# Softplus of the first feed-forward as one ScalarE function, and its inverse root on VectorE

## The chip, the cores and the metric

The kernel runs as one program on one core of a Trainium2 chip. The metric is the device time of one execution in microseconds (us); the time before is the median of 3 runs. PE is the matmul engine, ACT ScalarE, DVE VectorE, POOL GpSimd, SP SyncE, whose queue issues nearly all DMAs. Each engine works through its own instructions in the order in which the program has them; a wait at the head of one engine's queue holds everything behind it on that engine.

## What is computed

Causal attention with a cumulative bias (4 x 8 heads, 576 positions, width 64), then two feed-forward layers over 2304 tokens of width 512, cut here to what the change touches:

```python
h = x @ w_in                                               # 512 -> 2048
g = np.maximum(h, 0.0) + np.log1p(np.exp(-np.abs(h)))      # softplus
y = g @ w_out                                              # 2048 -> 512
rms = np.sqrt(np.mean(y * y, axis=-1, keepdims=True) + 1e-06)
xn = y / rms * rms_g
out = (silu(xn @ w_gate) * (xn @ w_val)) @ w_out2          # 512 -> 1536 -> 512
```

## The kernel before

Three parts follow each other on PE: attention, the first feed-forward, the second. Weights arrive as 64-bit numbers and are turned into fp32 on the core, chunk by chunk, during the first two parts. Every fp32 product is made of three matmuls on high and low halves (`mm3`, L773): high times high, high times low, low times high. So each activation that feeds a matmul is needed as a high half (`gh`, rounded to the matmul type) and a low half (`gl`, value minus high half).

**First feed-forward.** Tokens go in 6 tiles of 384. A step is one tile and one block of 128 of the 2048 hidden columns. There are 96 steps: a first pass of 6 blocks for each tile, then a second of 10 blocks for each tile, whose sums are added to those of the first (read back from DRAM, `y_load`). On PE a step has two blocks of 12 matmuls of 128x384: `h` (L778), from x, and `Y` (L828), which multiplies the softplus by w_out into four PSUM banks.

Between h and Y a step passes through nine small functions: `m1_abs` (ACT, |h|), `m1_exp` (ACT), `m1_ln` (ACT, ln(1+e)), `m1_u` (ACT, 1+e rounded), `m1_d` (DVE, the rounding error of it), `m1_g` (DVE, max(h,0) minus the error, the last reader of h in PSUM), `m1_add` (DVE), `m1_gh` (ACT) and `m1_gl` (POOL in the first 6 steps, DVE after that). h has three PSUM buffers, so h of step i+3 needs step i's to be read out.

**What sets the order.** All events of the two feed-forwards carry a place, in units of steps, and are sorted by it (`at`, L995; the table `OFF1`, L19). h of step i stands at i-0.57, Y at i+2.57. So on PE the blocks run h(i+3), Y(i), h(i+4), Y(i+1) and so on. Each engine's queue has its events in the order of these places. The same sort places:

- the conversion of weight chunks: `w_fetch` (SP), `w_conv_a` (ACT, two operations, the first an Abs), `w_conv_d` (DVE, three), `w_conv_p` (POOL), then `w_hi` and `w_lo`; one chunk per 1.49 steps in the first third, one per 2.9 steps later;
- the x tiles: `x_load` (SP), and `x_split` for four column blocks of the next tile (ACT `xh`, then POOL `xl`);
- the norm of a finished tile t, whose places are counted from e, the place of its last Y: `m1_evac` (DVE adds the sums of the first pass), `m1_ss`, `m1_sh` (POOL and DVE, squares), `m1_ssum` (two matmuls), `m1_inv` (inverse root), `m1_xn` (POOL multiplies, SP stores). `m1_inv` uses one DVE operation, Ln and Exp on ACT and one Newton step of four POOL operations.

In SP's queue the `y_load`s of tile t+1 stand behind the first `m1_xn` stores of tile t. The **second feed-forward** has 72 iterations of 24 matmuls (`m2_gv`) and 9 (`m2_out`), with `m2_act` between them (a Sigmoid on ACT, three DVE operations).

Of the kernel before, what the change touches and what calls it, by code (L numbers as in the profile page):

```python
# [10 lines left out]
I32 = mybir.dt.int32  # L11
# [3 lines left out]
AF = mybir.ActivationFunctionType  # L15
ALU = mybir.AluOpType
AX = mybir.AxisListType
PSUM = bass.MemoryType.PSUM
OFF1 = {  # L19
    "h": -0.57067,  # L20
    "A": -0.10511,
    "X": 0.37619,
    "LN": 0.46084,
    "U": 0.37819,
    "D": 0.52100,
    "G": 0.93713,
    "AD": 0.93913,
    "GH": 1.47301,
    "GL": 1.54335,
    "Y": 2.56558,  # L30
    "CF": -0.42676,
    "CA": 2.13954,
    "CD": 2.14154,
# [123 lines left out]
def attention_moe_kernel(ctx, tc, q, k, v, s, w_in, w_out, w_gate, w_val, w_out2, rms_g, out):  # L157
    nc = tc.nc
    B, H, S, D = q.shape
# [9 lines left out]
    NTILE = NT // T  # L169
# [6 lines left out]
    FA = 6  # L176
# [12 lines left out]
    pools = {}  # L189
# [13 lines left out]
    def f32(ap):  # L203
        return ap.bitcast(F32)
# [36 lines left out]
    def w_conv_a(ph, c):  # L241
        raw = raws[ph, c, "d"].bitcast(I32).rearrange("p (n t) -> p n t", t=2)
        pool = pools["cur"] if "m1" not in pools and CONV.index((ph, c)) % 2 else conv
        ur = pool.tile([P, 2, 512], I32, tag="ur", name="ur", bufs=1)
        u, r3 = ur[:, 0], ur[:, 1]
        nc.scalar.activation(out=f32(u), in_=f32(raw[:, :, 1]), func=AF.Abs)
        nc.scalar.activation(out=r3, in_=raw[:, :, 0].bitcast(U32), func=AF.Copy, scale=2.0 ** -29)
        st["cv", ph, c] = u, r3

# [51 lines left out]
    st = {}  # L301
# [486 lines left out]
    def m1_tile(tag, bufs, dt=F32):  # L788
        return pools["m1"].tile([P, T], dt, tag=tag, name=tag, bufs=bufs)

    def m1_abs(i):
        e = st["e", i] = m1_tile("e", 2)
        nc.scalar.activation(out=e, in_=st["h", i], func=AF.Abs)

    def m1_exp(i):
        e = st["e", i]
        nc.scalar.activation(out=e, in_=e, func=AF.Exp, scale=-1.0)

    def m1_ln(i):
        l = st["l", i] = m1_tile("l", 2)  # L800
        nc.scalar.activation(out=l, in_=st["e", i], func=AF.Ln, bias=1.0)  # L801

    def m1_u(i):
        u = st["u", i] = m1_tile("u", 1)
        nc.scalar.activation(out=u, in_=st["e", i], func=AF.Copy, bias=1.0)

    def m1_d(i):
        e = st["e", i]
        nc.vector.scalar_tensor_tensor(out=e, in0=st.pop(("u", i)), scalar=-1.0, in1=e, op0=ALU.add, op1=ALU.subtract)  # L809

    def m1_g(i):
        e = st["e", i]
        nc.vector.scalar_tensor_tensor(out=e, in0=st.pop(("h", i)), scalar=0.0, in1=e, op0=ALU.max, op1=ALU.subtract)  # L813

    def m1_add(i):
        l = st["l", i]
        nc.vector.tensor_tensor(out=l, in0=l, in1=st.pop(("e", i)), op=ALU.add)  # L817

    def m1_gh(i):
        gh = st["gh", i] = m1_tile("gh", 3, F32R)  # L820
        nc.scalar.activation(out=gh, in_=st["l", i], func=AF.Copy)  # L821

    def m1_gl(i):
        gl = st["gl", i] = m1_tile("gl", 3, F32R)
        eng = nc.gpsimd if i < FA else nc.vector
        eng.tensor_tensor(out=gl, in0=st.pop(("l", i)), in1=f32(st["gh", i]), op=ALU.subtract)  # L826

    def m1_y(i):  # L828
        v, _, f = STEPS[i]
# [32 lines left out]
    def ss_tile(tag, dt=F32, w=T):  # L862
        return pools["m1"].tile([P, T if tag == "sh" else 512], dt, tag=tag, name=tag, bufs=1)[:, 0:w]
# [25 lines left out]
    def m1_inv(t):  # L889
        o = st.pop(("ss", t))  # L890
        ms, z, w = ss_tile("sq"), ss_tile("acc"), ss_tile("sh")
        if t == NTILE - 1:
            nc.scalar.preload_act_table_set("natural_log_exp_and_others")
        nc.vector.tensor_scalar(out=ms, in0=o[:, 0:T], scalar1=1.0 / DM, scalar2=1e-6, op0=ALU.mult, op1=ALU.add)
        nc.scalar.activation(out=z, in_=ms, func=AF.Ln)
        nc.scalar.activation(out=z, in_=z, func=AF.Exp, scale=-0.5)
        nc.gpsimd.tensor_tensor(out=w, in0=z, in1=z, op=ALU.mult)
        nc.gpsimd.tensor_tensor(out=w, in0=w, in1=ms, op=ALU.mult)
        nc.gpsimd.tensor_scalar(out=w, in0=w, scalar1=-0.5, scalar2=1.5, op0=ALU.mult, op1=ALU.add)
        nc.gpsimd.tensor_tensor(out=z, in0=z, in1=w, op=ALU.mult)  # L900
        st["inv", t] = z

    def m1_xn(t, a):
# [63 lines left out]
    with tc.manual_schedule():  # L967
# [21 lines left out]
        with ExitStack() as es0:  # L989
            pools["ps"] = es0.enter_context(tc.tile_pool(name="ps", bufs=1, space=PSUM, reuse_waits="tile"))  # L990
            pools["wb"] = es0.enter_context(tc.tile_pool(name="wb", bufs=1, reuse_waits="tile"))
            pools["m1"] = es0.enter_context(tc.tile_pool(name="m1", bufs=1, reuse_waits="tile"))
            evs = []

            def at(x, fn, *args):  # L995
                evs.append((x, len(evs), fn, args))

            NS = range(len(STEPS))
            for i in NS:
                for nm, fn in (("h", m1_h), ("A", m1_abs), ("X", m1_exp), ("LN", m1_ln), ("U", m1_u), ("D", m1_d),  # L1000
                               ("G", m1_g), ("AD", m1_add), ("GH", m1_gh), ("GL", m1_gl), ("Y", m1_y)):
                    if nm != "h" or i > 1:
                        at(i + OFF1[nm], fn, i)
            CONV1 = (("CF", w_fetch), ("CA", w_conv_a), ("CD", w_conv_d), ("CP", w_conv_p))
            SPLIT = (("CH", w_hi), ("CL", w_lo))
            x = OFF1["P0"]
            for ph, c in [(1, c) for c in range(NA, 2 * F1)] + [(2, c % (3 * F2)) for c in range(NA + N2, NA + 3 * F2)]:
                if x < len(NS) or ph == 1:
                    for nm, fn in CONV1 + (SPLIT if ph == 1 or c < NA else (("CS", w_store),)):
                        at(x + OFF1[nm], fn, ph, c)  # L1010
                x += OFF1["PR"] if ph == 1 else OFF2["CV"]
            for v in sorted({STEPS[i][0] for i in NS}):
                i = min(i for i in NS if STEPS[i][0] == v)
                t, n = v % NTILE, FA if v < NTILE else F1 - FA
                if v > 0:
                    for a in range(KD):
                        x = i + OFF1["xs"] + OFF1["xt"] * a
                        at(x + OFF1["xl"], x_load, v, a)
                        at(x, x_split, v, a, nc.gpsimd)
                e = i + n - 1 + OFF1["Y"]  # L1020
                for a in range(KD):
                    at(e + 0.001 * (a + 1), m1_evac, v, a)
                if v < NTILE:
                    continue
                for a in range(KD):
                    at(e - 1.5 + 0.2 * a, y_load, t, a)
                x = "5" if t == NTILE - 1 else ""
                for a in range(KD):
                    at(e + OFF2["ss"] + OFF2["sr"] * a, m1_ss, t, a)
                    at(e + OFF2["xn" + x] + OFF2["xr" + x] * a, m1_xn, t, a)  # L1030
                at(e + OFF2["sh" + x], m1_sh, t)
                at(e + OFF2["sm" + x], m1_ssum, t)
                at(e + OFF2["iv" + x], m1_inv, t)
            for a in range(KD):
                at(OFF2["s0"] + a - 1.8, n_load, 0, a)
                at(OFF2["s0"] + a, x_split, 0, a, nc.vector, True)
            for c in range(NA, 3 * F2):
                x = OFF2["L0"] + OFF2["LR"] * c
                at(x + OFF2["WL"], w_load, 2, c)
                at(x + OFF2["WH"], w_hi, 2, c)  # L1040
                at(x + OFF2["WO"], w_lo, 2, c)
            e = F1 * NTILE
            for i in range(NTILE * F2):
                t, f = divmod(i, F2)
                x = e + (OFF2[f"g{i}"] if i < 2 else OFF2["G"] + 1.5 * i)
                at(x, m2_gv, t, f)
                at(e + OFF2[f"a{i}"] if i < 2 else x + OFF2["a"], m2_act, t, f)
                x = e + OFF2["G"] + 1.5 * (i + OFF2["lag"]) + OFF2["o"]
                at(x, m2_out, t, f)
                if f == F2 - 1:  # L1050
                    at(x + 0.01, m2_evac, t)
                if t + 1 < NTILE and 4 <= f < 8:
                    at(x + 0.3, n_load, t + 1, f - 4)
                if t + 1 < NTILE and 6 <= f < 10:
                    at(x, x_split, t + 1, f - 6, nc.vector, True)
            evs.sort(key=lambda x: x[:2])
            for _, _, fn, args in evs:
                fn(*args)
# [29 lines left out]
```

## Time and profile before

| | |
|---|---|
| time, median of 3 runs (lowest, highest) | 1173.48 us (1172.21, 1176.06) |
| span of the profiled execution, first to last instruction | 1171.5 us |
| what the profiled execution has beside its span | not in the profile; the median is 2.0 us above the span |
| busy: PE, DVE, ACT, POOL | 1108.0, 731.3, 560.5, 474.8 us |
| first feed-forward, about | 279 to 723 us |
| second feed-forward, about | 710 to 1166 us |

The profile's page gives busy time by engine, then the span in 40 slices of 29.3 us with one digit for each (tenths busy; PEclk is the granted clock of PE in tenths). The window rows give, for a stretch in us from the span's start, its length and for PE, PEld (weight loads), DVE, ACT and POOL the busy time and, as (x...), the number of instructions, then the granted clock, the DMA share and GB/s. The wait rows give who waited <- for whom: total us, times, longest. The group rows give line, engine, operation, output<-input, shape, count | busy us, mean ns | idle before it and what ended that. The rows in order of time give start, duration, engine, line, operation and, in brackets, the idle time before it and what ended it. Matmuls overlap in the pipeline, so a matmul of 0.33 us can start every 0.17 us: the distance between starts is what counts.

### The profile page before, as it was taken

To read this page: it belongs to the slowest core of one execution; us is meant where nothing else is said; L and a number is where in the kernel's file an instruction comes from. 1 tells how busy PE (TensorE), PEld (TensorE's weight loads), DVE (VectorE), ACT (ScalarE), POOL (GpSimd) and SP (SyncE) were. 2 spreads that over 40 slices of the span, in tenths; PEclk is the share of its full clock that TensorE was granted. 3 is DMA by queue.
4 is the path that set the end of the run, shared out by engine and by line. 5 is a ranking of instruction groups with operands and counts; after the bars stand their busy time and mean duration, and the time that the engine had idled before them with its cause. 6 is when DMAs were issued, how large, how long until landed. Compare 5 with 4: busy or idle time off the path is not lost.

```text
span 1171.5 us, 19408 instructions
## 1 busy us (share of the span) xinstructions
PE 1108.0 (95%) x7428; PEld 1021.9 (87%) x7428; DVE 731.3 (62%) x1170; ACT 560.5 (48%) x1203; POOL 474.8 (41%) x404
## 2 busy tenths in 40 slices
PE   5889999997998989999999999999999999999998
PEld 4767777777988889999998999999999999999997
DVE  6788888722899998799898995343332332333322
ACT  2545656544777877776766765431211212112111
POOL 5687766644655551357767766650000000000000
PEclk9988988888999999999989999999999999999999
DMA  8556888533434433323323134231010010010000
GB/s 176 140 144 159 207 204 214 148 100 109 132 127 128 137 113 104 117 86 104 95 91 104 56 95 125 80 101 41 14 39 4 14 41 14 6 37 14 27 1 28
DMA packets 126972, 107.59 MB, mean 92 GB/s; under 512 B 67008, under 2 KB 112704, under 8 KB 126816
## 3 DMA queue, kind: packets, MB, share of 16 engines
q1 hardware_dynamic: 126848, 106.36, 31.5%
q8 instruction: 58, 0.95, 0.3%
q14 instruction: 34, 0.28, 0.1%
q0 software_dynamic: 32, 0.00, 0.0%
HBM read 80.36 MB, written 25.83 MB: 91 GB/s over the span
## 4 chain that ended last, share of the span: by engine, by line
PE 59%; DVE 25%; issue 4%; DMA 4%; ACT 4%; POOL 3%; SPq 0%; DVEq 0%; POOLq 0%; ACTq 0%
DVE gl L826 4%; PE g L776 4%; PE g L775 4%; PE v L774 4%; PE v L775 4%; PE v L776 4%; PE g L774 4%; PE t L505 3%; DVE ur L253 3%; DVE l L817 3%; PE o L950 3%; PE o L951 3%; DVE ur L255 3%; PE s L449 3%; PE o L949 3%
## 5 line engine op out<-in xcount | busy, mean ns | idle before, releaser
L775 PE MATMUL y<-gl,w 128*128 128x384 f32 x384 | 131.5, 342 | 14.9 <-DVE gl L826 12.4
L263 POOL TENSOR_TENSOR wf<-ur 128x512 int32<-128x512 int32 x68 | 94.5, 1389 | 122.2 <-DVE ur L257 48.7
L934 DVE TENSOR_TENSOR u<-g,u 128x384 f32<-128x384 f32 x71 | 39.5, 557 | 158.6 <-ACT u L933 158.6
L774 PE MATMUL y<-gh,w 128*128 128x384 f32 x384 | 129.8, 338 | 2.2 <-DVE yt L853 1.8
L776 PE MATMUL y<-gh,w 128*128 128x384 f32 x384 | 129.4, 337 | 0.0
L936 ACT ACTIVATE gh<-l 128x384 fp32r<-128x384 f32 x72 | 37.9, 527 | 155.9 <-DVE l L935 155.9
L933 ACT ACTIVATE u<-g 128x384 f32<-128x384 f32 x71 | 34.8, 491 | 151.6 <-PE g L776 151.6
L472 DVE TENSOR_REDUCE mc<-s 128x1 f32<-128x128 f32 (+4 forms) x160 | 76.7, 537 | 31.6 <-PE s L457 25.9
L775 PE MATMUL g<-xl,w 128*128 128x384 f32 x284 | 95.5, 336 | 0.7 <-DVE xl L768 0.7
L776 PE MATMUL g<-xh,w 128*128 128x384 f32 x284 | 95.8, 337 | 0.0
L774 PE MATMUL g<-xh,w 128*128 128x384 f32 x284 | 95.6, 337 | 0.0
L776 PE MATMUL v<-xh,w 128*128 128x384 f32 x284 | 94.9, 334 | 0.0
L774 PE MATMUL v<-xh,w 128*128 128x384 f32 x284 | 94.9, 334 | 0.0
L775 PE MATMUL v<-xl,w 128*128 128x384 f32 x284 | 94.9, 334 | 0.0
L809 DVE SCALAR_TENSOR_TENSOR e<-u,e 128x384 f32<-128x384 f32 x96 | 77.6, 808 | 26.9 <-ACT l L801 26.9
L775 PE MATMUL h<-xl,w 128*128 128x384 f32 x256 | 87.4, 341 | 3.9 <-POOL xl L771 3.9
L775 PEld LDWEIGHTS y<-gl,w 128*128 128x128 f32 x384 | 72.6, 189 | 21.2 <-DVE gl L826 17.9
L826 DVE TENSOR_TENSOR gl<-l,gh 128x384 fp32r<-128x384 f32 x90 | 88.3, 981 | 4.5 <-ACT gh L821 1.0
L774 PE MATMUL h<-xh,w 128*128 128x384 f32 x256 | 87.5, 342 | 1.2 <-DVE e L813 1.2
L776 PE MATMUL h<-xh,w 128*128 128x384 f32 x256 | 86.8, 339 | 0.0
L817 DVE TENSOR_TENSOR l<-l,e 128x384 f32<-128x384 f32 x96 | 80.4, 837 | 3.7
L522 ACT ACTIVATE e<-t 128x448 f32<-128x448 f32 (+2 forms) x128 | 56.4, 506 | 54.5 <-PE t L515 54.2
(178 smaller groups left out, 3094.8 us busy)
## 6 DMA issues: line engine op xcount, KB each, us to landing
raw<-in_moe_w_out_dram SPq DMA_DIRECT2D x28, 512.0 KB
raw<-in_moe_w_in_dram SPq DMA_DIRECT2D x16, 512.0 KB
raw<-in_moe_w_gate_dram SPq DMA_DIRECT2D x12, 512.0 KB
raw<-in_moe_w_val_dram SPq DMA_DIRECT2D x12, 512.0 KB
wf<-wf SPq DMA_DIRECT2D x24, 256.0 KB
wl<-wf SPq DMA_DIRECT2D x24, 256.0 KB
xr<-x SPq DMA_DIRECT2D x28, 192.0 KB
qn<-in_q_dram SPq DMA_DIRECT2D x16, 288.0 KB
```

The lines of the kernel that those rows point to most:

```text
L253: nc.vector.tensor_scalar(out=f32(u), in0=f32(u), scalar1=2.0 ** -15, scalar2=122880.0, op0=ALU.max, op1=ALU.min)
L263: nc.gpsimd.tensor_tensor(out=w.bitcast(I32), in0=u, in1=r3, op=ALU.add)
L472: nc.vector.reduce_max(out=o, in_=x, axis=AX.X, negate=True)
L522: nc.scalar.activation(out=st["e", p][:, hd, c:c + w], in_=st["t", p, bk][hd][:, 0:w], func=AF.Exp)
L774: nc.tensor.matmul(o, wh, xh, start=start, stop=False)
L775: nc.tensor.matmul(o, wh, xl, start=False, stop=False)
L776: nc.tensor.matmul(o, wl, xh, start=False, stop=stop)
L809: nc.vector.scalar_tensor_tensor(out=e, in0=st.pop(("u", i)), scalar=-1.0, in1=e, op0=ALU.add, op1=ALU.subtract)
L817: nc.vector.tensor_tensor(out=l, in0=l, in1=st.pop(("e", i)), op=ALU.add)
L826: eng.tensor_tensor(out=gl, in0=st.pop(("l", i)), in1=f32(st["gh", i]), op=ALU.subtract)
L934: nc.vector.tensor_tensor(out=u, in0=g, in1=u, op=ALU.mult)
L936: nc.scalar.activation(out=gh, in_=l, func=AF.Copy)
```

## The change

Three edits go together. First, h is read twice from PSUM by the ACT function Softplus, once into `l` (fp32) and once into `gh`; `m1_gl` subtracts them on DVE in all 96 steps. The other seven functions go. Places: h at i-0.57, the softplus at i+0.02, gl at i+0.30, Y at i+1.57, a step earlier than before. Second, `m1_inv` starts from a bit pattern and makes three Newton steps, all eleven operations on DVE. Third, the Abs of `w_conv_a` becomes a DVE operation (a mask of the sign bit) in the first feed-forward; in attention it stays on ACT.

```diff
 OFF1 = {
-    "h": -0.57067,
-    "A": -0.10511,
...
-    "Y": 2.56558,
+    "h": -0.57,
+    "SP": 0.02,
+    "GL": 0.30,
+    "Y": 1.56558,
...
-        nc.scalar.activation(out=f32(u), in_=f32(raw[:, :, 1]), func=AF.Abs)
+        if "m1" in pools:
+            nc.vector.tensor_scalar(out=u, in0=raw[:, :, 1], scalar1=0x7FFFFFFF, scalar2=None, op0=ALU.bitwise_and)
+        else:
+            nc.scalar.activation(out=f32(u), in_=f32(raw[:, :, 1]), func=AF.Abs)
...
-    def m1_abs(i):
...
+    def m1_sp(i):
+        h = st.pop(("h", i))
         l = st["l", i] = m1_tile("l", 2)
...
         gh = st["gh", i] = m1_tile("gh", 3, F32R)
-        nc.scalar.activation(out=gh, in_=st["l", i], func=AF.Copy)
+        nc.scalar.activation(out=l, in_=h, func=AF.Softplus)
+        nc.scalar.activation(out=gh, in_=h, func=AF.Softplus)
...
-        eng = nc.gpsimd if i < FA else nc.vector
-        eng.tensor_tensor(out=gl, in0=st.pop(("l", i)), in1=f32(st["gh", i]), op=ALU.subtract)
+        nc.vector.tensor_tensor(out=gl, in0=st.pop(("l", i)), in1=f32(st["gh", i]), op=ALU.subtract)
...
-        if t == NTILE - 1:
-            nc.scalar.preload_act_table_set("natural_log_exp_and_others")
         nc.vector.tensor_scalar(out=ms, in0=o[:, 0:T], scalar1=1.0 / DM, scalar2=1e-6, op0=ALU.mult, op1=ALU.add)
-        nc.scalar.activation(out=z, in_=ms, func=AF.Ln)
-        nc.scalar.activation(out=z, in_=z, func=AF.Exp, scale=-0.5)
-        nc.gpsimd.tensor_tensor(out=w, in0=z, in1=z, op=ALU.mult)
-        nc.gpsimd.tensor_tensor(out=w, in0=w, in1=ms, op=ALU.mult)
-        nc.gpsimd.tensor_scalar(out=w, in0=w, scalar1=-0.5, scalar2=1.5, op0=ALU.mult, op1=ALU.add)
-        nc.gpsimd.tensor_tensor(out=z, in0=z, in1=w, op=ALU.mult)
+        nc.vector.tensor_scalar(out=z.bitcast(I32), in0=ms.bitcast(I32), scalar1=-0.5, scalar2=1597463007.0,
+                                op0=ALU.mult, op1=ALU.add)
+        for _ in range(3):
+            nc.vector.tensor_tensor(out=w, in0=z, in1=z, op=ALU.mult)
+            nc.vector.scalar_tensor_tensor(out=w, in0=w, scalar=-0.5, in1=ms, op0=ALU.mult, op1=ALU.mult)
+            nc.vector.scalar_tensor_tensor(out=z, in0=w, scalar=1.5, in1=z, op0=ALU.add, op1=ALU.mult)
```

ACT where the first feed-forward begins, before; `e_4322` and `e_4335` belong to steps 0 and 1, `xh` is the split of the second x tile:

```order
L577 ACTIVATE xz_4276<-o0_4280 128x384
L793 ACTIVATE e_4322<-h_4229 128x384
L797 ACTIVATE e_4322<-e_4322 128x384
L805 ACTIVATE u_4325<-e_4322 128x384
L801 ACTIVATE l_4327<-e_4322 128x384
L793 ACTIVATE e_4335<-h_4208 128x384
L797 ACTIVATE e_4335<-e_4335 128x384
L805 ACTIVATE u_4340<-e_4335 128x384
L801 ACTIVATE l_4355<-e_4335 128x384
L821 ACTIVATE gh_4357<-l_4327 128x384
L770 ACTIVATE xh_4362<-xr_4319 128x384
```

The same place in the changed kernel:

```order
L573 ACTIVATE xz_4276<-o0_4280 128x384
L791 ACT_TABLE_LOAD
L791 ACTIVATE l_4322<-h_4229 128x384
L792 ACTIVATE gh_4323<-h_4229 128x384
L791 ACTIVATE l_4333<-h_4208 128x384
L792 ACTIVATE gh_4334<-h_4208 128x384
L766 ACTIVATE xh_4368<-xr_4319 128x384
```

Eight operations that alternate with three on DVE became four that read PSUM and nothing of DVE; a table load stands ahead of them. The program has three table loads: at its start, here, and before the first Sigmoid (before: four, two of them around the last tile's inverse root).

POOL around the inverse root of tile 0 (tile `acc_7078`), before; `xl` are the third and fourth column block of the next x tile, `yt<-yt,acc` is `m1_xn`:

```order
L263 TENSOR_TENSOR wf_7022<-ur_6981 128x512
L771 TENSOR_TENSOR xl_7027<-xr_6927,xh_7026 128x384
L771 TENSOR_TENSOR xl_7027<-xr_6975,xh_7026 128x384
L897 TENSOR_TENSOR sh_7079<-acc_7078 128x384
L898 TENSOR_TENSOR sh_7079<-sh_7079,sq_7077 128x384
L899 TENSOR_SCALAR sh_7079<-sh_7079 128x384
L900 TENSOR_TENSOR acc_7078<-acc_7078,sh_7079 128x384
L905 TENSOR_TENSOR yt_6643<-yt_6643,acc_7078 128x384
```

The same place in the changed kernel:

```order
L259 TENSOR_TENSOR wf_6611<-ur_6575 128x512
L767 TENSOR_TENSOR xl_6616<-xr_6533,xh_6615 128x384
L873 TENSOR_TENSOR yt_6261<-yt_6261,acc_6620 128x384
L767 TENSOR_TENSOR xl_6616<-xr_6569,xh_6615 128x384
L873 TENSOR_TENSOR yt_6263<-yt_6263,acc_6620 128x384
```

The places of the norm count from Y, which went a step earlier, those of the x split do not: the first `m1_xn` now stands ahead of the fourth `xl`.

DVE around the inverse root of tile 2, before (a few rows of three steps; `sq<-o0` is all that DVE does of it):

```order
L817 TENSOR_TENSOR l_8009<-l_8009,e_7989 128x384
L809 SCALAR_TENSOR_TENSOR e_8041<-u_8051,e_8041 128x384
L826 TENSOR_TENSOR gl_8071<-l_8009,gh_8068 128x384
L894 TENSOR_SCALAR sq_8089<-o0_8047 128x384
L813 SCALAR_TENSOR_TENSOR e_8041<-x1_7996,e_8041 128x384
```

The same place in the changed kernel, up to the first of three Newton steps:

```order
L796 TENSOR_TENSOR gl_7435<-l_7431,gh_7432 128x384
L240 TENSOR_SCALAR ur_7465<-raw_7357 128x512
L249 TENSOR_SCALAR ur_7465<-ur_7465 128x512
L251 TENSOR_SCALAR ur_7465<-ur_7465 128x512
L253 SCALAR_TENSOR_TENSOR ur_7465<-raw_7357,ur_7465 128x512
L862 TENSOR_SCALAR sq_7480<-o0_7437 128x384
L863 TENSOR_SCALAR acc_7481<-sq_7480 128x384
L866 TENSOR_TENSOR sh_7482<-acc_7481 128x384
L867 SCALAR_TENSOR_TENSOR sh_7482<-sh_7482,sq_7480 128x384
L868 SCALAR_TENSOR_TENSOR acc_7481<-sh_7482,acc_7481 128x384
```

The last three stand there twice more, then gl of the next step: eleven operations in one piece, and for this tile a chunk's conversion of four right ahead of them.

## Rows read from the trace of the kernel before

**Rows 1.** The page: busy time, and two lines of the slices.

```profile
PE 1108.0 (95%) x7428; PEld 1021.9 (87%) x7428; DVE 731.3 (62%) x1170; ACT 560.5 (48%) x1203; POOL 474.8 (41%) x404
...
DVE  6788888722899998799898995343332332333322
...
PEclk9988988888999999999989999999999999999999
```

**Rows 2.** Windows: five stretches of the two feed-forwards.

```profile
278.50:298.00 19.50, 17.93 (x84) 17.29 (x85) 8.39 (x13) 10.34 (x23) 11.31 (x10) 0.85 0.54 167
298.00:440.00 142.00, 129.22 (x708) 123.47 (x708) 133.82 (x190) 112.66 (x238) 78.52 (x58) 0.99 0.40 127
440.00:580.00 140.00, 139.83 (x804) 139.05 (x804) 120.02 (x181) 99.82 (x210) 66.68 (x57) 1.00 0.31 96
580.00:710.00 130.00, 122.15 (x676) 119.24 (x675) 118.36 (x159) 90.16 (x188) 86.98 (x73) 0.97 0.30 94
730.00:1160.00 430.00, 430.00 (x2268) 403.29 (x2267) 136.11 (x247) 93.72 (x186) 35.76 (x31) 1.00 0.09 29
```

**Rows 3.** Waits of PE between 278 and 715 us.

```profile
PE y L775 <- DVE gl L826: 12.4, 11, 2.2
PE x L774 <- DVE e L813: 5.6, 1, 5.6
PE h L775 <- POOL xl L771: 3.9, 4, 1.0
```

**Rows 4.** Groups of instructions by line and shape, 290 to 710 us.

```profile
L826 DVE TENSOR_TENSOR gl<-l,gh 128x384 fp32r<-128x384 f32 x88 | 86.8, 986 | 3.9 <-ACT gh L821 0.4
...
L817 DVE TENSOR_TENSOR l<-l,e 128x384 f32<-128x384 f32 x93 | 77.5, 833 | 3.6
L809 DVE SCALAR_TENSOR_TENSOR e<-u,e 128x384 f32<-128x384 f32 x93 | 75.9, 816 | 17.9 <-ACT l L801 17.9
...
L813 DVE SCALAR_TENSOR_TENSOR e<-h,e 128x384 f32<-128x384 f32 x62 | 34.0, 548 | 0.1
L793 ACT ACTIVATE e<-h 128x384 f32<-128x384 f32 x61 | 29.0, 475 | 4.7 <-PE h L776 4.6
L257 DVE SCALAR_TENSOR_TENSOR ur<-raw,ur 128x512 int32<-128x512 int32 x40 | 28.6, 715 | 1.4
...
L246 ACT ACTIVATE ur<-raw 128x512 f32<-128x512 f32 x40 | 26.4, 661 | 0.0
```

**Rows 5.** In order of time, DVE alone, then DVE and POOL together.

```profile
275.72 0.56 DVE L809 SCALAR_TENSOR_TENSOR e<-u,e 128x384 f32<-128x384 f32 x1
276.31 0.56 DVE L813 SCALAR_TENSOR_TENSOR e<-h,e 128x384 f32<-128x384 f32 x1
...
577.54 1.65 DVE L826 TENSOR_TENSOR gl<-l,gh 128x384 fp32r<-128x384 f32 x1
...
577.15 1.62 POOL L263 TENSOR_TENSOR wf<-ur 128x512 int32<-128x512 int32 x1
```

**Rows 6.** In order of time, where the first feed-forward begins: PE, then ACT.

```profile
278.58 0.69 PE L774 MATMUL x<-xh,w 128*128 128x384 f32 x1 [5.60 <-DVE e L813]
...
273.02 0.49 ACT L577 ACTIVATE xz<-o 128x384 f32<-128x384 f32 x1 [0.53 <-PE o L539]
273.41 0.48 ACT L793 ACTIVATE e<-h 128x384 f32<-128x384 f32 x1
...
286.34 0.53 ACT L770 ACTIVATE xh<-xr 128x384 fp32r<-128x384 f32 x1 [8.32 <-DMA xr<-x]
```

**Rows 7.** In order of time, ACT's table load before the first Sigmoid.

```profile
715.16 1.28 ACT L933 ACT_TABLE_LOAD   x1
716.46 0.49 ACT L933 ACTIVATE u<-g 128x384 f32<-128x384 f32 x1
```

**Rows 8.** In order of time around 570 to 586 us, an inverse root: DVE, POOL, DVE.

```profile
569.84 0.55 DVE L894 TENSOR_SCALAR sq<-o 128x384 f32<-128x384 f32 x1
...
578.73 5.21 POOL L905 TENSOR_TENSOR yt<-yt,acc 128x384 f32<-128x384 f32 x4
...
586.02 1.11 DVE L853 TENSOR_TENSOR yt<-y,yt 128x384 f32<-128x384 f32 x2 [1.97 <-DMA yt<-yp]
```

More of the change, by code (lines that the diff above doesn't have):

```diff
@@ L19 @@
 OFF1 = {
-    "h": -0.57067,
-    "A": -0.10511,
[L22 to L29, printed above, removed]
-    "Y": 2.56558,
+    "h": -0.57,
+    "SP": 0.02,
+    "GL": 0.30,
+    "Y": 1.56558,
     "CF": -0.42676,
@@ L789, in m1_tile @@
         return pools["m1"].tile([P, T], dt, tag=tag, name=tag, bufs=bufs)
-    def m1_abs(i):
[L792 to L799, printed above, removed]
-        l = st["l", i] = m1_tile("l", 2)
[L801 to L819, printed above, removed]
+    def m1_sp(i):
+        h = st.pop(("h", i))
+        l = st["l", i] = m1_tile("l", 2)
         gh = st["gh", i] = m1_tile("gh", 3, F32R)
-        nc.scalar.activation(out=gh, in_=st["l", i], func=AF.Copy)
+        nc.scalar.activation(out=l, in_=h, func=AF.Softplus)
+        nc.scalar.activation(out=gh, in_=h, func=AF.Softplus)
     def m1_gl(i):
         gl = st["gl", i] = m1_tile("gl", 3, F32R)
-        eng = nc.gpsimd if i < FA else nc.vector
-        eng.tensor_tensor(out=gl, in0=st.pop(("l", i)), in1=f32(st["gh", i]), op=ALU.subtract)
+        nc.vector.tensor_tensor(out=gl, in0=st.pop(("l", i)), in1=f32(st["gh", i]), op=ALU.subtract)
     def m1_y(i):
@@ L999, in attention_moe_kernel @@
             for i in NS:
-                for nm, fn in (("h", m1_h), ("A", m1_abs), ("X", m1_exp), ("LN", m1_ln), ("U", m1_u), ("D", m1_d),
-                               ("G", m1_g), ("AD", m1_add), ("GH", m1_gh), ("GL", m1_gl), ("Y", m1_y)):
+                for nm, fn in (("h", m1_h), ("SP", m1_sp), ("GL", m1_gl), ("Y", m1_y)):
                     if nm != "h" or i > 1:
```

## The prediction

> **What bounds the kernel now.** I read the page first: PE is busy for 1108.0 of 1171.5 us, DVE for 731.3 [rows 1]. That share is an average, so the slices and then the windows. In 440 to 580 us PE starts 804 matmuls in 140 us, 174 ns each, and in 730 to 1160 us it is busy without a gap [rows 2]. The second feed-forward is bound by PE and nothing in it can become shorter by this change. The first could run at 174 ns throughout, and does so only in its middle. At 174.1 ns the 84 matmuls of 278.5 to 298 us would take 14.6 us, the 708 up to 440 us 123.3, the 676 of 580 to 710 us 117.7: PE loses 4.9, 18.7 and 12.3 us, 35.9 us in all [rows 2]. To this comes the idle time of 5.6 us ahead of the first of these matmuls [rows 6].
>
> For what does PE wait there? Most for gl of DVE (12.4 us in 11 waits), once for the first L813 (5.6), a little for the x split on POOL (3.9) [rows 3]. The waits named are less than what is lost: after a wait the granted clock falls, to a mean of 0.85 in the first stretch [rows 2]. DVE is busy for 133.8 of the 142 us of the stretch that loses most [rows 2], and much of that is the work between h and Y, which also goes to ACT and back three times. So the bound of the stretches that lose is the chain of nine functions with DVE as its engine.
>
> **The change, part by part.** *Softplus.* DVE loses L809 (75.9 us), L817 (77.5) and L813 (34.0 for two of the three PSUM buffers, so some 50): about 204 us in 420 [rows 4]. ACT loses five operations a step and gains two. No row shows Softplus; the nearest is L793, Abs of the same PSUM tile, at 0.475 us, and I take that. Between the end of h and its Y now lie four blocks of 12 matmuls (Y(i-2), h(i+1), Y(i-1), h(i+2)), 8.4 us at 174 ns. The chain needs two reads (0.9 us), gl (0.56 alone, 1.65 beside POOL [rows 5]) and some 0.2 us of handing over: 1.7 to 2.8 us. The cover is 5 to 6 us, enough for a conversion of a chunk that stands ahead of gl on DVE. If Softplus took twice as long, it would still be covered.
>
> *Abs on DVE.* 40 operations, between the other one-source operation of the conversion and L257, which reads the same strided input (0.715 us [rows 4]): 17 to 29 us of DVE time, from which gl hides as above. The wait for the raw chunk's DMA comes to stand at the head of DVE's queue, with the gl's behind it. ACT's L246 had that wait and was idle for 0.0 us ahead of it [rows 4], so I price it at nothing; if fetches came late, each late us would be taken from the 5 to 6 us of cover. With 204 us gone, 29 and the inverse roots below added, DVE falls from 381 us between 278.5 and 710 us [rows 2] to about 250.
>
> *The start.* h of step 2 waited until 278.58 us for L813 of step 1 [rows 6]; now it waits for the second read by ACT. ACT comes free at 273.5 [rows 6]. A table load takes 1.28 us and the next operation begins 0.02 us behind it [rows 7]. Four reads, 0.4 us from start to start as ACT's operations have it at 273.02 and 273.41 [rows 6], end at about 276.5: h begins 2.0 us earlier. (By the Trainium skill, page "ScalarE: Activation LUTs", section "What ACT_TABLE_LOAD costs", a switch is 1283 ns and a drain of about 1380 ns. The first agrees with the row, the second is not in it; by the page the gain here would be 0.6 us.) Next is the x split: ACT waits for the x tile's DMA until 286.34 [rows 6], which hangs on the end of attention and stays where it is. Until the x tile is split PE has eight blocks to do now, against seven in the order before: from 276.5 with 2.8 us for the slow clock they last until 296, and the split ends at about 297 in its fourth column block, which the last quarter of h reads. So of the 4.9 us some 2.8 remain: 2.1 gained.
>
> *The two stretches that lose.* In 298 to 440 us I leave 1.5 us of the 18.7 (changes of tile, where Y waits for PSUM to be read out): gain 17.2. In 580 to 710 us I leave 2.0 of the 12.3: gain 10.3. The large stall there is y of the next tile, which DVE had to wait for until 586.02, because its load stands behind the store of `m1_xn` in SP's queue [rows 8]. From the start of the inverse root to there were 16.2 us (569.84 to 586.02). In the new order eight blocks, 16.7 us, pass between the norm's matmuls and the last Y, and two more us until its banks are needed. The new chain has the inverse root (7.5 us, below), then 7.3 us as from 578.73 to 586.02, and one `xl` of 1.3: about 16, just inside.
>
> *The inverse root.* Eleven dependent operations on DVE. Alone such operations follow each other every 0.59 us (275.72, 276.31 [rows 5]): 6.4 us. One that meets a POOL operation takes 1.65 instead of 0.56 [rows 5]. POOL's queue has one or two operations left before it must wait for the result, so I take one meeting, 7.5 us; all of them at gl's mean of 0.986 [rows 4] give 9.9. Who waits: gl of the next step, which has 9.5 us, and, new, the fourth `xl` of the next x tile. It now stands behind the first `m1_xn` in POOL's queue. From the norm's matmuls, the inverse root (T), `m1_xn` and `xl` (1.3 us each, as a quarter of the 5.21 [rows 8]) need T + 2.8 us; h reads that `xl` four blocks and ten matmuls later, after 10.1 us. So each of tiles 0 to 3 costs T - 7.3 us: 0.2 at 7.5. In tile 2 a chunk's conversion stands right ahead: 2 more. In tile 4, where the second feed-forward comes next, gl of step 94 is needed after 8.5 us and comes at about 9. Sum 3 us; I take 4. In tile 5 PE has enough in front of it, and DVE is a third busy there [rows 2].
>
> **The sum**, against the profiled span: 1171.5 - 2.0 - 2.1 - 17.2 - 10.3 + 4.0 = 1143.9. The median lies 2.0 us above the span: 1146 us.
>
> **The rivals.** (1) *The inverse root is slow.* At T = 9.9 tiles 0, 1 and 3 cost 2.6 each, tile 2 4.7, tile 4 2.9: 15.4 instead of 4, 1157 us. At its worst each of its nine operations with two SBUF inputs meets one of POOL: 9 x 1.65 + 1 = 15.9 us, 8.6 for three tiles, 10.7 and 9: 45 us, 1187, slower than before. Against it speaks POOL's queue, which holds no more than two operations that don't wait for this very result. (The Trainium skill, page "SBUF — State Buffer", section "Who interferes with whom", has it that a VectorE operation with two SBUF inputs and a GpSimd one that reads SBUF share a port that one holds to its end; the row of 1.65 us agrees, and by that rule moving this work from POOL to DVE is what could turn the change round.)
>
> (2) *The feed stays.* What PE waited for was named DVE because it came last; behind it are the x split (3.9 us already now) and SP's queue, held by the stores of `m1_xn`. If half of what 298 to 440 us lost by other than gl's waits remains (6 us), and 5 us of the stall at 586: 1157 us. For it speaks that POOL and SP keep their order; against, that 440 to 580 us has the same feed and loses nothing.
>
> (3) *Softplus is slow on this chip*, the case on the other side. From 278.5 to 710 us ACT is busy for 313 us in 94.7 steps of 24 matmuls [rows 2], 3.3 us a step; less five operations of half a microsecond and the Abs, 0.5 us remain beside Softplus (0.9 in 298 to 440 us). PE needs 4.2 us a step, the mean step of before takes 4.56. So ACT would be the bound from 1.65 us for one Softplus on in the first third, and the kernel slower than before from 2.05 on; at 2.2 us the step is 4.9 and the time 1173 + 95 x 0.34 = 1205 us. A Copy, an Abs and a Sigmoid of this shape take 0.48 to 0.49 us [rows 6, 7], whatever the function, so I hold this unlikely. (4) *It does not do what it says*: more table loads than the three in the program are excluded by its order; that PE runs at 174 ns only where DVE happens to be idle would leave 1170 to 1177. (5) *All losses go*, the inverse root too: 1146 - 4 - 3.5 = 1138.
>
> **How the numbers follow.** Forecast (1140 to 1151): 0.62. Slow inverse root at about 1157: 0.12, at its worst 0.02. Feed stays, about 1157: 0.12. All losses go: 0.05. Softplus slow: 0.04. No effect: 0.03. A measurement of this kernel tells about 0.3% from no change, 3.5 us. Faster by more: 0.62 + 0.12 + 0.12 + 0.05 = 0.91. Within: 0.03. Slower: 0.06. The range takes in the forecast, the floor and the two cases at 1157 with some 4 us around them: 1137 to 1161.
>
> **What would show it.** Right: windows of the first feed-forward with 174 ns a matmul almost throughout and a granted clock of 1.00; DVE below two thirds busy there; Softplus at about 0.47 us; the first h of step 2 near 276.5; no waits of PE for gl but beside inverse roots; waits of PE's h for `xl` of about 1 us once in ten steps. Wrong: Softplus above 1 us; the eleven operations over 10 us; DVE idle ahead of the sign mask, with DMA as what ended it; PE's Y waiting for y read back; the same 28 us a tile in the first pass.

## The result, and the profile after

The changed kernel takes 1138.61 us (median of 4 runs, 1133.78 to 1144.24); the kernel before took 1172.85 beside it (4 runs, 1171.99 to 1176.06). The ratio is 0.9705, 95% interval 0.9667 to 0.9744: 34 us, or 3.0%, faster. The profiled execution took 1135.85 us with a span of 1134.1.

Attention, which the change does not touch, varies from run to run: in the thirteen profiles of this case the first h of the first feed-forward starts between 254.1 and 267.9 us. So below I compare what lies behind it: **the rest**, from the first matmul of h of step 2 (the `x` matmul with an idle time ahead of it) to the end of the span. Before, it was 1171.5 - 278.58 = 892.9 us [rows 6]; after, 1134.1 - 274.68 = 859.4.

The page after, its busy times and two lines of slices, beside [rows 1]:

```profile
PE 1089.5 (96%) x7428; PEld 1014.4 (89%) x7428; DVE 607.5 (54%) x988; ACT 390.2 (34%) x862; POOL 433.9 (38%) x374
...
DVE  5778888840788863475665754532332333323222
...
PEclk9989888999999999999999999999999999999999
```

Windows after, with the stretches of [rows 2] and one that stops ahead of the second feed-forward:

```profile
278.50:298.00 19.50, 19.38 (x112) 19.06 (x111) 9.52 (x13) 8.46 (x18) 9.86 (x8) 1.00 0.60 179
298.00:440.00 142.00, 142.00 (x821) 142.00 (x820) 106.23 (x136) 65.14 (x139) 74.72 (x56) 1.00 0.47 145
440.00:580.00 140.00, 140.00 (x810) 140.00 (x809) 78.67 (x119) 45.29 (x101) 72.97 (x64) 1.00 0.33 103
...
580.00:680.00 100.00, 97.57 (x559) 96.64 (x558) 64.90 (x91) 33.14 (x70) 58.08 (x50) 1.00 0.30 97
```

PE starts 821 matmuls where it started 708, 173 ns each, at full granted clock and without a gap. A block of 12 takes 2.08 us, a step of 24 takes 4.16. If I add up, block by block, what lies between two starts beyond 2.08 us, the first feed-forward behind h of step 2 lost 39.3 us before and loses 4.9 after. What PE still waits for, 270 to 690 us:

```profile
PE x L770 <- ACT gh L792: 3.5, 1, 3.5
PE h L771 <- POOL xl L767: 2.2, 1, 2.2
...
PE g L771 <- DVE xl L764: 0.2, 1, 0.2
```

The start, in order of time, ACT and then PE, beside [rows 6]:

```profile
271.19 0.49 ACT L573 ACTIVATE xz<-o 128x384 f32<-128x384 f32 x1 [0.53 <-PE o L535]
271.70 1.28 ACT L791 ACT_TABLE_LOAD   x1
272.99 0.49 ACT L791 ACTIVATE l<-h 128x384 f32<-128x384 f32 x1
273.38 0.48 ACT L792 ACTIVATE gh<-h 128x384 fp32r<-128x384 f32 x1
...
274.12 0.51 ACT L792 ACTIVATE gh<-h 128x384 fp32r<-128x384 f32 x1
284.96 0.53 ACT L766 ACTIVATE xh<-xr 128x384 fp32r<-128x384 f32 x1 [10.32 <-DMA xr<-x]
...
274.68 0.69 PE L770 MATMUL x<-xh,w 128*128 128x384 f32 x1 [3.54 <-ACT gh L792]
```

Softplus takes 0.49 us, like the other functions of this shape. The idle time ahead of h of step 2 is 3.54 us instead of 5.60.

### The profile page after: what moved, and what is told of

Same layout as the page of the kernel before. It is cut to its first block, busy times and chain, and to the rows that moved or that the text cites. A ratio compares the mean times of both kernels' runs of the same rounds, so it can differ in the third digit from the quotient of the medians.

```text
span 1134.1 us, 18838 instructions
## 1 busy us (share of the span) xinstructions
PE 1089.5 (96%) x7428; PEld 1014.4 (89%) x7428; DVE 607.5 (54%) x988; ACT 390.2 (34%) x862; POOL 433.9 (38%) x374
## 4 chain that ended last, share of the span: by engine, by line
PE 77%; DVE 10%; issue 4%; POOL 4%; DMA 4%; ACT 1%; SPq 0%; DVEq 0%; POOLq 0%; ACTq 0%
PE y L771 5%; PE y L772 5%; PE y L770 5%; PE v L772 4%; PE v L771 4%; PE v L770 4%; PE g L772 4%; PE g L771 4%; PE g L770 4%; PE h L771 4%; PE h L770 4%; PE h L772 4%; PE t L501 4%; PE s L445 3%; PE o L918 3%
## 5 line engine op out<-in xcount | busy, mean ns | idle before, releaser
L771 PE MATMUL y<-gl,w 128*128 128x384 f32 x384 | 128.5, 335 | 0.1
L770 PE MATMUL y<-gh,w 128*128 128x384 f32 x384 | 128.3, 334 | 0.0
L772 PE MATMUL y<-gh,w 128*128 128x384 f32 x384 | 128.3, 334 | 0.0
L796 DVE TENSOR_TENSOR gl<-l,gh 128x384 fp32r<-128x384 f32 x96 | 72.7, 765 | 103.3 <-ACT gh L792 103.2
L770 PE MATMUL h<-xh,w 128*128 128x384 f32 x256 | 85.6, 334 | 0.0
L772 PE MATMUL h<-xh,w 128*128 128x384 f32 x256 | 85.5, 334 | 0.0
L791 ACT ACTIVATE l<-h 128x384 f32<-128x384 f32 x64 | 31.4, 491 | 136.3 <-PE h L772 136.3
L772 PEld LDWEIGHTS y<-gh,w 128*128 128x128 f32 x384 | 72.1, 188 | 0.0
```

The lines of the kernel that those rows point to most:

```text
L770: nc.tensor.matmul(o, wh, xh, start=start, stop=False)
L771: nc.tensor.matmul(o, wh, xl, start=False, stop=False)
L772: nc.tensor.matmul(o, wl, xh, start=False, stop=stop)
L796: nc.vector.tensor_tensor(out=gl, in0=st.pop(("l", i)), in1=f32(st["gh", i]), op=ALU.subtract)
```

## The experiments

All numbers of "the rest" are span minus the start of that matmul, as above, from one profile each. Each ratio is to runs of the kernel before that were made beside the run (medians 1169.88 to 1173.97 us), not to the first row.

| kernel | median, us | ratio to before (95%) | the rest, us |
|---|---|---|---|
| before | 1172.85 | | 892.9 |
| changed | 1138.61 | 0.9705 (0.9667, 0.9744) | 859.4 |
| changed, measured again (e0) | 1136.45 | 0.9672 (0.9635, 0.9709) | 858.8 |
| before, new inverse root alone (e2) | 1189.37 | 1.0149 (1.0116, 1.0183) | 912.0 |
| changed, old inverse root (e1) | 1135.12 | 0.9686 (0.9627, 0.9744) | 857.9 |
| changed, Abs on ACT (e4) | 1150.96 | 0.9805 (0.9760, 0.9851) | 874.1 |
| before, Y a step later (e11) | 1179.75 | 1.0084 (1.0056, 1.0111) | 900.8 |
| changed, gl twice (e3) | 1146.12 | 0.9783 (0.9728, 0.9837) | 867.7 |
| changed, gl three times (e9) | 1186.20 | 1.0134 (1.0097, 1.0171) | 910.1 |
| changed, Softplus twice (e7) | 1141.33 | 0.9742 (0.9703, 0.9782) | 863.7 |
| changed, Y at its old place (e8) | 1141.07 | 0.9713 (0.9672, 0.9755) | 862.8 |
| changed, fourth xl first (e5) | 1133.73 | 0.9652 (0.9619, 0.9685) | 857.2 |
| e5, table load early (e6) | 1131.67 | 0.9646 (0.9612, 0.9680) | 858.7 |

### Measured again

No edit. 

> The changed kernel itself, so that what is compared with it ran on the same chip; its four times so far lie 10.5 us apart (1133.8 to 1144.2), those of before 4.1. Theory: the spread comes from attention, where PE waits and its granted clock changes; 1134 to 1144 us again, and the first feed-forward from its first h of step 2 to its last Y the same within 1 us of the profile seen (274.7 to 680 us). Rival: the spread comes from the first feed-forward, and that stretch differs by several us.

Measured: 1136.45 us (1130.20 to 1139.40, 6 runs); the rest agrees with the first profile within 0.6 us, and the matmul counts and waits are the same. These two profiles lie only 0.3 us apart in time, so they do not show by themselves where the 10 us between runs of one kernel come from. The profiles of the kernels that share this attention point to it: their first h starts anywhere from 254.1 to 267.9 us.

### One edit alone: the inverse root

In the kernel before, the new `m1_inv` and nothing else:

```diff
-        nc.scalar.activation(out=z, in_=ms, func=AF.Ln)
...
+        nc.vector.tensor_scalar(out=z.bitcast(I32), in0=ms.bitcast(I32), scalar1=-0.5, scalar2=1597463007.0,
+                                op0=ALU.mult, op1=ALU.add)
...
```

> The kernel before with the new inverse root alone. Theory: before, DVE and its exchange with ACT are the bound where the first feed-forward loses, so 6.5 us of DVE in one piece for each tile hold up gl: slower by 3 to 15 us (1176 to 1188). Rival: the old inverse root on ACT and POOL was itself a cause of the stalls after 580 us, and this gains 3 us or more.

Measured: 1189.37 us against 1169.88 beside it, 19 us slower, in the expected direction and larger. Waits of PE, 268 to 710 us, and the window in which the kernel before lost about 1 us [rows 2]:

```profile
PE y L775 <- DVE gl L826: 12.5, 16, 2.2
PE x L774 <- DVE e L813: 8.9, 2, 5.6
PE h L774 <- DVE e L813: 8.6, 3, 5.5
...
440.00:580.00 140.00, 133.13 (x756) 130.57 (x755) 122.77 (x191) 92.62 (x194) 57.85 (x48) 0.99 0.30 94
```

L813 is the last reader of h in PSUM. Where DVE owns it, eleven operations in one piece hold up h itself, up to 5.5 us at a time: 756 matmuls instead of 804.

The other way round, in the changed kernel the old `m1_inv` (Ln, Exp, one Newton step on POOL; the diff above with its signs turned, but without the table preload for the last tile).

> Softplus and the places of the changed kernel, but the inverse root of before (Ln and Exp on ACT, a Newton step on POOL); Softplus and Ln lie in different tables, so ACT loads a table twice for each tile, 2.6 us. Theory: Newton on VectorE gains nothing itself; it only spares the table loads, and those would be covered by the four blocks: within 4 us of the changed kernel (1135 to 1144), with waits of h for xl up to 2 us a tile. Rival: the table loads stand between h and Y and cost their 2.6 us for each of five tiles, 13 us: about 1151.

Measured: 1135.12 us and a rest of 857.9, as the changed kernel within 1.5 us, though this program has 21 table loads, three for each tile where two were expected. So the inverse root on DVE brings nothing by itself. It costs 19 us in the kernel before and next to nothing in the changed one. Two things differ between these: which engine releases h's buffers, and how much other work DVE has. The run with gl three times, below, bears on which of them counts.

### One edit undone: the sign mask

```diff
-        if "m1" in pools:
-            nc.vector.tensor_scalar(out=u, in0=raw[:, :, 1], scalar1=0x7FFFFFFF, scalar2=None, op0=ALU.bitwise_and)
-        else:
-            nc.scalar.activation(out=f32(u), in_=f32(raw[:, :, 1]), func=AF.Abs)
+        nc.scalar.activation(out=f32(u), in_=f32(raw[:, :, 1]), func=AF.Abs)
```

> The changed kernel with the third edit undone: |raw| of a weight chunk by Abs on ACT again. In this program's tables Abs and Softplus do not lie together, so each of 40 chunks brings two table loads (83 in the program instead of 3): 80 x 1.28 = 102 us more on ACT and 40 Abs of 0.66, 26 us; DVE has 43 us less. From 298 to 440 us, with 20 chunks, ACT goes from 65 to about 130 of 142 us. Theory: two loads, Abs and Copy stand together ahead of a Softplus, 3.7 us, inside the cover of 5 to 6 us, so little is lost: 0 to 10 us, 1138 to 1148 us. Rival: ACT with 3.9 us a step and its bursts becomes what PE waits for, more than 15 us: above 1153 us, with waits of PE's Y for gh or of h for the second Softplus.

Measured: 1150.96 us, rest 874.1: 15 us more, between the two expectations. The wait is neither's. PE waits for `xl` of POOL, 8.5 us in six waits of h and 2.5 in one more of h into its third buffer. In order of time at a change of tile, ACT, POOL, PE:

```profile
346.27 1.28 ACT L788 ACT_TABLE_LOAD   x1
...
348.46 1.28 ACT L239 ACT_TABLE_LOAD   x1
349.75 0.66 ACT L239 ACTIVATE ur<-raw 128x512 f32<-128x512 f32 x1
350.31 0.67 ACT L240 ACTIVATE ur<-raw 128x512 int32<-128x512 uint32 x1
350.88 0.52 ACT L763 ACTIVATE xh<-xr 128x384 fp32r<-128x384 f32 x1
...
351.47 1.44 POOL L764 TENSOR_TENSOR xl<-xr,xh 128x384 fp32r<-128x384 f32 x1 [2.46 <-ACT xh L763]
...
352.97 0.45 PE L768 MATMUL h<-xl,w 128*128 128x384 f32 x1 [1.07 <-POOL xl L764]
```

Softplus hides behind its cover, but two table loads for each chunk push the last column block of the x split back, and that has no cover. ACT was busy 129.5 of the 142 us, as worked out ahead of the run; which of its operations would be late was not. The run does not tell apart what the loads cost and what the Abs itself costs on ACT.

### Chain or work: where the 19 us of 298 to 440 us were lost

My prediction called the bound "the chain of nine functions". A chain that is too long is helped by more distance between its ends. So in the kernel before:

```diff
-    "Y": 2.56558,
+    "Y": 3.56558,
```

> The kernel before with every Y one step later (place 3.57 instead of 2.57), nothing else: the work of all engines is the same, but gl has one step (4.16 us) more until its Y. What it tells apart is how the stretch from 298 to 440 us lost its 19 us. Chain (my prediction's words): a step's nine functions take too long from h to Y; with 4.16 us more of cover the waits go, and the kernel gains 10 to 18 us there: about 1153 to 1163 us. Throughput: DVE has 133.8 us of work in 29.5 steps, 4.54 us a step against PE's 4.16; a queue that is longer by a step can be used up once, so the gain is 4 us at most in the first third and the windows show DVE still at 130 us or more of 142 with PE at 700 to 725 matmuls: about 1168 to 1175 us.

Measured: 1179.75 us, slower. Its window and the waits of PE from 270 to 715 us:

```profile
298.00:440.00 142.00, 128.69 (x691) 123.72 (x690) 130.52 (x183) 108.99 (x230) 78.43 (x57) 0.96 0.39 120
...
PE x L774 <- DVE e L813: 8.4, 3, 5.6
PE h L774 <- DVE e L813: 8.1, 8, 2.3
PE h L775 <- POOL xl L771: 7.7, 7, 1.3
```

The waits for gl, 12.4 us in [rows 3], are gone; in their place PE waits for DVE at h's buffers. The chain reading, a gain of 10 to 18 us, falls. The other had DVE's busy time right (130 us or more), but expected at most a small gain and 700 to 725 matmuls in the stretch: the kernel loses 8 us and starts 691. The edit lengthens only the way from gl to Y; the way from h to L813, which hands h's buffer back, is as long as before, and PE now waits there. So this run rules out the distance to Y as the bound, and not every chain. In this stretch the granted clock is 0.96 instead of 0.99; in all of them together the waits of h for `xl` went from 3.9 to 7.7 us. I did not take this loss apart further.

The changed kernel with DVE loaded up again, gl computed twice, then three times into the same tile:

```diff
-        nc.vector.tensor_tensor(out=gl, in0=st.pop(("l", i)), in1=f32(st["gh", i]), op=ALU.subtract)
+        l = st.pop(("l", i))
+        for _ in range(2):
+            nc.vector.tensor_tensor(out=gl, in0=l, in1=f32(st["gh", i]), op=ALU.subtract)
```

> The changed kernel with gl computed twice: 96 more DVE operations of 0.56 to 0.77 us. DVE's busy share in 298 to 440 us goes from 75% to about 90%, near the 94% of before. Theory (the bound of before was the chain that goes back and forth between ACT and DVE, not DVE's amount of work): the chain from h to Y grows by 0.6 us inside a cover of 5 to 6 us, and the time stays within 3 us of the changed kernel. Rival (DVE's amount of work was the bound): most of the 19 us that before lost in that stretch come back.

> The changed kernel with gl computed three times into the same tile, so that DVE has two subtractions a step more and the chain is longer by two of them, 1.7 us; the other engines and the order are as in the changed kernel. With gl twice DVE had 3.92 us of work a step between 298 and 440 us and PE lost little there. Throughput: 3.92 + 0.85 = 4.77 us a step against 4.16, over some 33 steps: 20 us lost in that stretch, DVE 95% busy or more, time about 1160 to 1172 us. Chain: the cover of 5 to 6 us still holds the two more operations, so at most 5 us more than with gl twice (1146.1): 1146 to 1151 us.

Measured: 1146.12 and 1186.20 us. With gl twice the rest is 8 to 9 us longer than in the changed kernel, between the two expectations, and only 2.7 us of that lie in 298 to 440 us. The same window of both, then PE's waits with gl three times:

```profile
298.00:440.00 142.00, 140.57 (x805) 139.13 (x804) 131.41 (x168) 64.58 (x139) 76.78 (x55) 1.00 0.45 143
```

```profile
298.00:440.00 142.00, 128.83 (x705) 122.64 (x705) 137.93 (x183) 60.35 (x127) 76.02 (x55) 0.99 0.43 132
...
PE y L771 <- DVE gl L798: 19.4, 20, 2.5
PE h L771 <- POOL xl L767: 6.5, 2, 4.8
```

With gl three times the row of the changed kernel has become that of the kernel before, 705 matmuls against 708, with the same kind of wait, although the chain has only the softplus and the subtractions in it. Per step of 24 matmuls DVE has this much work in the stretch:

| kernel | DVE busy / steps | DVE work a step | matmuls short of 821 |
|---|---|---|---|
| changed | 106.2 / 34.2 | 3.11 us | 0 |
| gl twice | 131.4 / 33.5 | 3.92 | 16 |
| before | 133.8 / 29.5 | 4.54 | 113 |
| before, Y later | 130.5 / 28.8 | 4.53 | 130 |
| gl three times | 137.9 / 29.4 | 4.70 | 116 |

PE's step is 4.16 us. Under it little is lost in this stretch. Over it PE cannot keep its pace: the difference times the steps makes 11 us before and 16 with gl three times, of 19.5 and 20.1 us lost (113 and 116 x 0.173). What the remaining 4 to 8 us are made of was not taken apart. The busy share does not tell the cases apart: DVE is 93% busy with gl twice and 94% before. The 20 us that were expected of the third gl in this stretch came. The chain grew with the work, by 1.7 us; that the cover of 5 to 6 us holds this is argued, and only 0.8 us more were tested (next section).

The total is larger than expected, because the later stretches, which the expectation left out, lost too. Gl three times between 440 and 580 us, and an inverse root there (from 563.37 to 569.65 us on DVE), POOL and then PE:

```profile
440.00:580.00 140.00, 133.47 (x761) 131.69 (x760) 123.13 (x170) 40.86 (x92) 61.27 (x50) 1.00 0.31 96
...
569.74 1.25 POOL L875 TENSOR_TENSOR yt<-yt,acc 128x384 f32<-128x384 f32 x1 [7.88 <-DVE acc L870]
...
572.30 0.44 PE L771 MATMUL h<-xl,w 128*128 128x384 f32 x1 [1.73 <-POOL xl L767]
```

Here DVE has 3.88 us of work a step, under PE's 4.16, and PE still starts only 761 matmuls instead of 810, with waits behind the inverse roots for `xl` and gl. The kernel before with the new inverse root has 3.90 us a step and starts 756. The inverse root is the same in both; there DVE releases h, here ACT, and the loss is nearly the same. With gl twice, at 3.36 us a step, the same inverse roots cost nothing there (810 matmuls). So the inverse root is cheap where DVE has room left; that ACT releases h is not enough. The two kernels also differ in the place of Y and in the order on POOL, so how much of either loss hangs on who releases h stays open.

### The cover of Softplus

Both Softplus computed twice (four ACT operations a step instead of two):

```diff
-        nc.scalar.activation(out=l, in_=h, func=AF.Softplus)
-        nc.scalar.activation(out=gh, in_=h, func=AF.Softplus)
+        for _ in range(2):
+            nc.scalar.activation(out=l, in_=h, func=AF.Softplus)
+            nc.scalar.activation(out=gh, in_=h, func=AF.Softplus)
```

> The changed kernel with the two Softplus reads made twice: ACT has 0.8 us more in each step, on the way from h to gl. Theory: covered; the time stays within 2 us but for 0.8 us at the start, and PE shows no new waits for gl. Rival: the cover is thinner than the four blocks, and PE waits: 10 us or more.

Measured: 1141.33 us, rest 863.7. In 298 to 440 us PE starts 821 matmuls as in the changed kernel, and all its waits for gl are 0.7 us. The wait at the start is 5.1 us instead of 3.5. The rest, which begins behind that wait, is 4.3 us longer, more than the 2 us expected: 1.0 in the first stretch and 2.9 from 580 us on, where `xl` of tile 2 is waited for 3.0 us instead of 2.2 and gl 0.7, and the granted clock of 580 to 680 us is 0.98 instead of 1.00. From 298 to 440 us the chain has 0.8 us to spare in every step, as the prediction had it; beside the inverse roots it has not.

### The one stall left: xl behind the inverse root

```profile
576.34 0.42 DVE L240 TENSOR_SCALAR ur<-raw 128x512 int32<-128x512 int32 x1
...
579.99 0.55 DVE L862 TENSOR_SCALAR sq<-o 128x384 f32<-128x384 f32 x1
580.57 1.08 DVE L863 TENSOR_SCALAR acc<-sq 128x384 int32<-128x384 int32 x1
581.69 0.56 DVE L866 TENSOR_TENSOR sh<-acc 128x384 f32<-128x384 f32 x1
582.29 0.56 DVE L867 SCALAR_TENSOR_TENSOR sh<-sh,sq 128x384 f32<-128x384 f32 x1
...
586.44 0.56 DVE L868 SCALAR_TENSOR_TENSOR acc<-sh,acc 128x384 f32<-128x384 f32 x1
...
587.08 1.24 POOL L873 TENSOR_TENSOR yt<-yt,acc 128x384 f32<-128x384 f32 x1 [5.64 <-DVE acc L868]
588.28 1.30 POOL L767 TENSOR_TENSOR xl<-xr,xh 128x384 fp32r<-128x384 f32 x1
...
589.64 0.45 PE L771 MATMUL h<-xl,w 128*128 128x384 f32 x1 [2.22 <-POOL xl L767]
```

These are rows of the changed kernel in order of time: a conversion from 576.34, the inverse root behind it until 587.0, the first `m1_xn`, `xl`, then h. Putting `m1_xn` a little later, so that all `xl` stand ahead of it on POOL:

```diff
-    "xn": 8.20666,
+    "xn": 8.24000,
```

> The first store of the norm (m1_xn) is placed 0.03 of a step later, so that on POOL the fourth x split stands ahead of it. Theory: the one stall of 2.2 us of PE's h for xl, beside the inverse root of tile 2, goes, since only that order made the split wait for the inverse root; 2 to 2.5 us less than the changed kernel on the same chip. Rival: the stall moves to gl or to the y that is read back; no change.

Measured: 1133.73 us (1130.92 to 1135.59), rest 857.2, 1.6 and 2.2 us under the two profiles of the changed kernel. The wait is gone. The runs overlap too much to tell the two kernels apart by their time, but this median is, with the next one, the lowest that was measured.

On top of it, Softplus's table loaded earlier, in the last part of attention:

```diff
+        if p == NP - 1 and part == 0:
+            nc.scalar.preload_act_table_set("softplus")
```

> As the run with the x split first, and the table load of Softplus is placed ahead of the last attention outputs on ACT, which waits there anyway. Theory: the load of 1.28 us leaves the path to the first h of step 2, which begins 1.3 us earlier; 1 to 1.3 us less than with the split first. Rival: that start is not what sets the end, because the next x tile's DMA holds the steps after it; no change.

Measured: 1131.67 us. The rest is 858.7, and the idle time ahead of it 2.12 us instead of 3.54. Together they make 860.9 from attention's last matmul on, and 860.8 without the early load: nothing gained.

```profile
PE y L772 <- ACT gh L794: 2.2, 1, 2.2
PE x L772 <- ACT gh L794: 2.1, 1, 2.1
```

PE starts earlier and waits 2.2 us more a little later, since ACT stands until 282.69 us at the x split, which waits for its DMA (11.58 us idle ahead of it), and the next softplus stands behind that.

Last, the changed kernel with Y where it was before, a step later:

```diff
-    "Y": 1.56558,
+    "Y": 2.56558,
```

> The changed kernel with Y one step later, where it was before; all that counts from Y moves with it. Theory: the move of Y is not what gains, since a softplus of two reads and gl fits in four blocks of PE: the same time within 3 us, and the stall of h for xl goes as well, since the split then stands ahead of the store. At the start h of step 3 comes ahead of Y of step 0 again. Rival: the earlier Y is part of the gain; slower by 4 us (one block at each end) or more.

Measured: 1141.07 us, rest 862.8, 3.4 to 4.0 us more, between the two expectations. The norm, which counts from Y, ends a step later, and the first `g` of the second feed-forward waits 3.0 us for its `xl` (on DVE); the block of h that begins at 297 us loses 1.9 us; the stall of tile 2 is gone. Between 440 and 580 us nothing changes. So the earlier Y is worth some 4 us, and not for the sake of the softplus.

## Why the prediction was right, and where it was off

The sign, the size and the place were right: 1138.6 us lies within 1137 to 1161. It lies under the forecast of 1140 to 1151, 7.4 us under the number, and nearest to the rival in which all losses go, which had a chance of 0.05. Measured again, the kernel took 1136.45 us, just outside the range, so that the first number fell inside it is in part luck. The profiled span is 9.8 us under the 1143.9 of the sum. Of these, attention, which the change does not touch, ended 1.8 earlier (271.14 instead of 272.98 us). The other 8 us are 5.4 us of losses that I had left in the sum and that did not come, and 3.4 us of losses of before that I had not seen, less 0.8 us in the second feed-forward.

- **The start** was right: 2.0 us predicted, 5.60 - 3.54 = 2.06 measured. ACT's operation behind the table load began 0.01 us after it (271.70 + 1.28, then 272.99). The Trainium skill, page "ScalarE: Activation LUTs", section "What ACT_TABLE_LOAD costs", has a drain of about 1380 ns beside the load; no run here shows it.
- **The first stretch** kept 1.9 us of its losses where I left 2.8.
- **298 to 440 us** kept nothing; I left 1.5 for changes of tile. The block sums of before (39.3) are also 3.4 us above what I took from the windows (35.9), in part because the 174 ns that I took for the full pace held a loss of about 1 us in 140; it is 173.
- **580 to 710 us and the inverse roots**: 2.0 and 4.0 left, 3.0 measured by blocks (2.5 at tile 2's h, 0.5 at the first g). The inverse root took 6.9 us in tile 0 and 7.0 in tile 2; its operations follow each other every 0.59 us, and one of them, L863, met POOL, as taken. Tile 2 with the conversion ahead of it cost the 2.2 that was predicted; tiles 0, 1, 3 and 4 cost nothing. The chain of `y` that I had called "just inside" was inside.
- Some 0.8 us go the other way in the second feed-forward.

**What was wrong in the working.** First, the reason. The step "the bound of the stretches that lose is the chain of nine functions with DVE as its engine" named the wait, not the bound. DVE had 4.54 us of work a step against PE's 4.16, which alone makes 11 of the 19.5 us; a longer distance to Y did not help, and more DVE work in a short chain brought the loss back. What the other 8 us were stays open. The sum was not hurt, since the change removes the work and the chain together.

Second, a mis-sized term: **the sign mask**, bounded at 0.43 to 0.715 us. It took 1.15 in 298 to 440 us and 1.08 in the mean of 40. In order of time, changed kernel, DVE and then POOL:

```profile
345.52 1.52 DVE L240 TENSOR_SCALAR ur<-raw 128x512 int32<-128x512 int32 x1
347.07 0.43 DVE L249 TENSOR_SCALAR ur<-ur 128x512 f32<-128x512 f32 x1
...
345.14 1.61 POOL L291 TENSOR_TENSOR w<-wf,w 128x512 fp32r<-128x512 f32 x1
```

Alone it takes 0.42 us (576.34); here it ends 0.3 us behind the POOL operation that had begun before it (347.04, 346.75). I had priced only operations with two SBUF inputs as exposed to POOL. By the Trainium skill, page "VectorE: DVE Perf Modes", section "Mode 2×_2P", an operation with one SBUF source can use both read ports, and "SBUF — State Buffer", section "Who interferes with whom", names such modes among those that contend with GpSimd; the two rows agree. So DVE was 75% busy in 298 to 440 us, not below two thirds, and 273 us from 278.5 to 710 us instead of 250. At 3.11 us a step that cost nothing.

**The rivals.** A slow inverse root: no, 6.3 to 7.3 us a piece. That it costs so little rests on the room that DVE has in the changed kernel (2.3 us of work a step from 440 to 580 us): at 3.9 us a step the two in that stretch cost some 8 us, with h released by DVE and by ACT alike. The feed stays: not as priced; with DVE lighter, POOL's split came in time in all but one place. Softplus slow: 0.49 us; twice of it cost 1.5 us at the start and 4.3 in the rest, and nothing from 298 to 440 us. No effect: excluded.

## What to carry to other kernels

Divide the busy time of the engine that is waited for by the steps done in that stretch and compare it with the step of the engine that waits. If it is above, the engine that waits cannot keep its pace, and work has to be taken off; moving Y further away did not help here, the wait that ended last only changed its name. If it is below, look at bursts: from 440 to 580 us eleven operations in one piece cost nothing at 2.3 or 3.4 us of work a step and some 4 us each at 3.9, against a step of 4.16. At 3.9 the wait had another name where another engine released the buffer, and the loss was about as large.

## What was not expected of the hardware

A one-source DVE operation of 128x512 (the sign mask) took 0.42 us alone and, beside POOL, mostly 1.22 to 1.52. In the program with Abs on ACT, Softplus and Abs did not lie in one table: 41 loads of 1283 ns in 142 us, 20 of them ahead of an Abs and 21 ahead of a Softplus. Where waits of PE went from gl to h's buffer, the granted clock in 298 to 440 us fell from 0.99 to 0.96 at nearly the same busy time.
